# A band mask on the tensor engine: narrow local units of a four-layer attention kernel, with a re-searched instruction order

## The chip, the core and the metric

The kernel runs on one core of one Trainium2 chip. The core has a matrix engine (PE, with its weight loads shown apart as PEld), a vector engine (DVE), a scalar engine (ACT), a general engine (POOL) and a queue that issues transfers (SP). The metric is the device time of one execution in microseconds; smaller is better. Times are the median of the runs.

## The reference

Four layers act on one sequence of 2,048 tokens of 512 features: a local layer A, a global layer B, and both again with the same weights. Both have 32 heads of 16 features.

```
x = x + A(layernorm(x))      # A: W, dil = 8, 2: token i sees keys i, i-2, ..., i-14
x = x + B(layernorm(x))      # B: one shared K and V of 16 features, all 2048 keys, softmax
x = x + A(layernorm(x))
x = x + B(layernorm(x))

A: idx = pos[:, None] - arange(8) * 2;  logits = where(idx >= 0, q.k * 16**-0.5, -1e9)
   o = softmax(logits) @ v;  return o @ wo
B: return softmax(q @ k.T * 16**-0.5) @ v @ wo
```

The output has the shape and type of x, (1, 2048, 512) in bf16.

## The kernel before

**The global layers** are most of the work. Their scores are cut into 4,096 tiles of 128 keys by 512 queries. PE computes four tiles at a time, each on 32 of its rows (`score`, line 2534), and leaves them in PSUM. A tile then goes one of two ways. On the ACT way two tiles make one exponential (`exp`, line 2549, written to `pt`), and PE multiplies each by the values once. On the DVE way the tile is converted to integers (`copy`, line 2553, written to `t`), POOL makes two shifted versions of it (`do_pass`, line 2559, written to `i` and `i_pair`), and PE multiplies all three by scaled values. These products (`pv`, line 2570, written to `o`) use PE in four column strips side by side. So a tile on the ACT way costs PE one score and one product, and a tile on the DVE way one score and three products. There are two PSUM slots for scores on the ACT way, and at most two banks for scores on the DVE way.

**The local layers** are cut by token chunk (four chunks `c` of 512 tokens) and by half of a chunk (`kd`). Tokens of equal parity are neighbours, so the eight keys of a query lie in a band. The first two chunks of the first layer use wide units (72 key columns; they stay as they are). All others use narrow units: 48 of them, each with four heads on each 64-row half of PE, for eight blocks of 40 query columns, `UN` = 320 columns for each half. A narrow unit (`narrow_scores`) is 16 or 18 small score products into one PSUM slot (line 2455), one exponential on ACT (line 2463, written to `units`), and one AND on DVE that zeroes what lies outside the band (line 2469). In the first local layer every unit is finished by itself (`narrow_unit`). In the second, four units are finished together (`narrow_half`): PE sums the masked exponentials of the four (`total`, line 2386, written to `dn`), ACT takes the logarithm (line 2400) and an exponential (line 2402, both in `half`), the result goes out and back by transfer, and only then come the products with the values (line 2421). There are eight such groups.

**The order** of all instructions on all engines is fixed when the program is built. A planner (`Sched`, `Stream`) plays through the kernel with assumed durations (`MM`, `SWITCH`, `LAT`, the numbers given to `self.op`) and picks next what has the lowest key: its start plus weights. The weights are in `PRM`, `BIAS` and, for each of the 96 parts of the global layers, in the table `PHASES`. `FETCH` and `BLOCK` are the planner's limit on how fast PE gets its instructions. Each engine then runs its list in order and waits where data is missing. Where the plan leaves PE idle for long, it inserts products of zeros (`keep_awake`, line 1883).

Of the kernel before, what the change touches and what calls it, by code (L numbers as in the profile page):

```python
# [6 lines left out]
BF16 = mybir.dt.bfloat16  # L7
# [23 lines left out]
NJ = 3  # L31
# [379 lines left out]
def outproj_tm(ctx, tc, o_tm, wo_sb, x_sb, ident, S, tag):  # L411
# [5 lines left out]
    for qt in range(NT):  # L417
# [11 lines left out]
MM, SWITCH, DMA = 216.0, 96.0, 620.0  # L429
# [6 lines left out]
SENT, WALL, BLOCK, FETCH, REFILL = 45.0, 200.0, 255.55, 3050.0, 10.0  # L436
# [13 lines left out]
        "add": 223.2, "add_y": -114.7, "c2": -211.4, "c3": -91.88, "c6": 83.79, "c7": 14.68, "dve": -147.3,  # L450
        "ex": -306.6, "p0": -110.5, "sc": -133, "v1": -5823, "vcopy": 131.3, "vp": 291.7, "wpa": -0.02812,
    }, {
        "aq": -134.4, "dq": 158.3, "exq": -40.72, "mmi": 26.69, "mmq": 1.383, "nt": 46.85, "pv_in": 203.8,
        "slotv": -22.13, "vech": -0.2155,
    }, (77430, 20.0)),
    1: ({
        "act": 389.9, "add": 235.5, "add_y": -114.7, "c2": -211.4, "c3": -91.88, "dve": -147.3, "ex": -306.6,
        "p0": -110.5, "sc": -133, "vp": 291.7,
    }, {
        "aq": -134.4, "dq": 158.3, "exq": -40.72, "mmi": 26.69, "mmq": 1.383, "nt": 46.85, "open": 106.2,  # L460
        "pv_in": 203.8, "slotv": 1.595,
    }, (76143, 80.0)),
    2: ({
        "add": 235.5, "c0": -315, "c1": -201.2, "c3": -129.8, "c4": 4.013, "dve": -178.1, "evacX": 22.86, "ex": -306.6,
        "mm_b": -3091, "norm": 173.2, "recip": 151.1, "sc": -151.8, "see_b": 20390, "vp": 290.4, "wa": -0.1622,
    }, {
        "aq": -128.7, "dq": 159.2, "mmi": 51.61, "pv": 275.5, "vech": -0.2556, "vecp": -93.34,
    }, (48860, 160.0)),
    3: ({
        "add": 235.5, "c0": -315, "c1": -201.2, "c3": -129.8, "c4": 4.013, "dve": -178.1, "evacX": 22.86, "ex": -306.6,  # L470
        "mm_b": -3091, "norm": 173.2, "recip": 151.1, "sc": -151.8, "see_b": 20390, "vp": 290.4, "wa": -0.1622,
    }, {
        "aq": -128.7, "dq": 159.2, "mmi": 51.61, "pv": 275.5, "vech": -0.2556, "vecp": -93.34,
    }, (89741, 160.0)),
    4: ({
        "add": 96.11, "age": 0.03249, "c2": -189, "c6": 33.96, "evacX": 85.36, "ln": -136.1, "mask": 27, "mm_a": 202.8,
        "sc": -255.2, "turn": 31.66, "vcopy": 134.5, "vfirst": -1171,
    }, {
        "closing": 564.3, "few": 21.46, "mmi": 39.37, "ni": -30.74, "vec": 414.1,
    }, (95515, 160.0)),  # L480
    5: ({
        "aexp": -88.89, "age": 0.04278, "c1": -193.6, "c2": -145.8, "c4": -10.63, "c5": 114.5, "evac": 2514,
        "mm_b": -2741, "sc": -341.5, "turn_ev": -522.8, "wd": 0.03593, "wipe": 12860, "zer": -131.6,
    }, {
        "acth": 0.01482, "copy": 88.93, "dq": 10.2, "mmi": 48.87, "npt": 13.85, "pv_in": 70.63, "vecp": -61.26,
    }, (93829, 160.0)),
    6: ({
        "aexp": -88.89, "age": 0.04278, "c1": -193.6, "c2": -145.8, "c5": 114.5, "evac": 2514, "mm_b": -2741,
        "pad": -219200, "sc": -341.5, "turn_ev": -413.6, "wd": 0.03593, "wipe": 12860, "zer": -131.6,
    }, {  # L490
        "acth": 0.01482, "closing": 607.9, "copy": 88.93, "dq": 10.2, "mmi": 48.87, "npt": 13.85, "pv_in": 70.63,
    }, (11912, 160.0)),
    7: ({
        "aexp": -88.89, "age": 0.04278, "c1": -193.6, "c2": -145.8, "c5": 114.5, "evac": 2514, "mm_b": -2741,
        "pad": -219200, "sc": -341.5, "see": -217.3, "turn_ev": -413.6, "wd": 0.03593, "wipe": 12860, "zer": -131.6,
    }, {
        "acth": 0.01482, "closing": 607.9, "copy": 88.93, "dq": 10.2, "mmi": 48.87, "npt": 13.85, "pv_in": 70.63,
    }, (28948, 80.0)),
    8: ({
        "age": 0.05331, "away": -123.6, "c1": -362, "c6": 73.59, "dve": -144.6, "ln": -75.93, "mm_a": 399.4,  # L500
        "p0": -159.8, "pad": -219400, "see": -352.5, "st": -1643, "turn_ev": -423.9,
    }, {
        "aux": -5.231, "dq": 22.63, "mmi": 4.008, "mmpt": 17.28, "mmq": 13.92, "nt": 19.69, "pv": 282.5,
    }, (76363, 160.0)),
    9: ({
        "age": 0.05331, "away": -123.6, "c1": -362, "dve": -144.6, "mm_a": 399.4, "norm": 346.8, "pad": -219400,
        "see": -352.5, "st": -1643, "turn_ev": -423.9,
    }, {
        "copy": 73.55, "dq": 22.63, "mmi": 4.008, "mmpt": 17.28, "mmq": 13.92, "nt": 19.69, "pv": 282.5, "vecp": -61.45,
    }, (21942, 160.0)),  # L510
    10: ({
        "age": 0.05331, "c7": 39.95, "dmat": -84.43, "ln": -119, "on": 82.68, "p1": -6187, "recip": 124.2, "sc": -195.7,
        "split": -6952, "st": -1978, "turn": 52.13, "vcopy": 133.3, "vp": 61.75, "wpa": -0.01191,
    }, {
        "act": -83.47, "acth": -0.1093, "copy": 101.4, "mmi": 4.008, "mmpt": 12.19, "nt": -25.91, "pv": 216.7,
        "vecp": -57.25,
    }, (28571, 160.0)),
    11: ({
        "aexp": -73.39, "back": 1022, "c0": -186, "c3": -167.9, "dn": -21630, "mm_a": 222.2, "mm_b": -3007,
        "pad": -219500, "split": -7307, "turn_ev": -529.1, "v1": -5878, "wd": 0.189, "wpd": 0.1129, "zer": -389.9,  # L520
    }, {
        "aq": 19.81, "aux": -147.2, "mmi": -6.329, "pv": 195.3, "vec": 495.7, "vec2": 217.1, "vech": 0.1986,
    }, (63034, 8.0)),
    12: ({
        "back": 1023, "c0": -186, "c2": -182.3, "c6": 63.11, "dve": -78.77, "mm_a": 222.2, "mm_b": -3007,
        "split": -7428, "st": -1712, "v1": -5878, "wd": 0.09754, "wpd": -0.1118,
    }, {
        "aq": 19.81, "aux": -147.2, "exq": -79.78, "mmi": -6.329, "pv_in": 289.8, "vec": 517, "vec2": 147.3,
        "vech": 0.1395, "vecp": -52.17,
    }, (75059, 8.0)),  # L530
    13: ({
        "act": 248.2, "aggr": -3061, "away": -110.8, "c4": 8.258, "recip": 115.6, "split": -7535, "turn": 27.13,
        "v1": -6423, "vcopy": 152.3, "vp": 58.75, "wpa": -0.05655, "zer": -411.2,
    }, {
        "act": -142.3, "aq": -48.62, "few": 56.89, "pv_in": 207, "slotv": 35.96, "vech": -0.1282, "vecp": -65.6,
    }, (30282, 80.0)),
    14: ({
        "act": 248.2, "aexp": -50.83, "c1": -184.2, "c5": 142, "dmat": -59.08, "evacX": 72.81, "split": -7535,
        "turn": 27.13, "vcopy": 164.7, "wipe": 12740, "wpd": -0.06679,
    }, {  # L540
        "aq": -48.62, "aux": -8.007, "few": 56.89, "mmq": -15.71, "pv_in": 207, "slotv": 35.96,
    }, (33337, 160.0)),
    15: ({
        "add": 115.5, "age": 0.03159, "back": 144.4, "c7": 42.5, "dn": -21140, "dve": -56.65, "evac": 2855,
# [621 lines left out]
def act_ns(cols, pointers=0):  # L1166
    return 52.0 + 0.833 * cols + 93.0 * pointers
# [1888 lines left out]
```

## Time and profile before

| | |
|---|---|
| median of 3 runs | 1376.43 us (1375.53 to 1377.28) |
| the profiled execution | 1378.18 us, of which the span of the trace is 1376.0 us |
| mean granted clock of PE | 0.995 |
| busy | PE 97%, ACT 95%, DVE 93%, POOL 68% |

The rows further down are from the profiled execution. A busy PE is not a PE at its peak, since its products overlap; its pace is read from the starts of its instructions. The columns of a timeline are start and duration in microseconds, engine, line, operation, operands (out<-in), count, and in brackets the idle time before it and what ended it.

### The profile page before, as it was taken

To read this page: it belongs to the slowest core of one execution; us is meant where nothing else is said; L and a number is where in the kernel's file an instruction comes from. 1 tells how busy PE (TensorE), PEld (TensorE's weight loads), DVE (VectorE), ACT (ScalarE), POOL (GpSimd) and SP (SyncE) were. 2 spreads that over 40 slices of the span, in tenths; PEclk is the share of its full clock that TensorE was granted. 3 is DMA by queue.
4 is the path that set the end of the run, shared out by engine and by line. 5 is a ranking of instruction groups with operands and counts; after the bars stand their busy time and mean duration, and the time that the engine had idled before them with its cause. 6 is when DMAs were issued, how large, how long until landed. Compare 5 with 4: busy or idle time off the path is not lost. (4 is left out here: it accounts for less than half of the span.)

```text
span 1376.0 us, 48011 instructions
## 1 busy us (share of the span) xinstructions
PE 1341.6 (97%) x19604; PEld 459.4 (33%) x19606; DVE 1286.4 (93%) x2254; ACT 1311.4 (95%) x1549; POOL 929.2 (68%) x1226
## 2 busy tenths in 40 slices
PE   8999999999999999999999999999999999999997
PEld 5534243222223322433224334322222222222222
DVE  7987868999998899999998898999999999999998
ACT  6998989999999999999999998999999999999996
POOL 5126456787657567785677646877877678887884
PEclk9999999999999999999999999999999999999999
DMA  5012223011113110210113122221112200001000
GB/s 157 7 40 59 53 53 68 24 40 37 41 38 51 27 41 18 39 23 23 29 28 44 51 48 46 64 63 36 35 47 63 67 24 14 14 14 44 13 14 27
DMA packets 120876, 55.79 MB, mean 41 GB/s; under 512 B 98440, under 2 KB 104712, under 8 KB 120648
## 3 DMA queue, kind: packets, MB, share of 16 engines
q1 hardware_dynamic: 119784, 50.82, 15.9%
q8 instruction: 155, 2.54, 0.8%
q10 hardware_dynamic: 864, 1.84, 0.4%
q14 instruction: 73, 0.60, 0.1%
HBM read 27.10 MB, written 11.52 MB: 28 GB/s over the span
## 5 line engine op out<-in xcount | busy, mean ns | idle before, releaser
L2549 ACT ACTIVATE pt<-st 128x1024 bf16<-128x1024 f32 x1281 | 1196.3, 1121 | 27.1 <-PE dv L2534 12.3
L2553 DVE TENSOR_SCALAR t<-dv 128x512 int16<-128x512 f32 x1534 | 956.0, 680 | 34.0 <-PE dv L2534 24.7
L2559 POOL INT64_ADD i<-t x613 | 502.5, 825 | 245.5 <-DVE t L2553 102.3
L2559 POOL INT64_ADD i_pair<-t x411 | 337.7, 825 | 154.7 <-DVE t L2553 65.5
L2570 PE MATMUL o<-pt,VEa 128*32 128x512 bf16 x1308 | 260.7, 387 | 0.1
L2570 PE MATMUL o<-pt,region 128*32 128x512 bf16 x1254 | 259.6, 385 | 0.0
L2534 PE MATMUL st<-QT,KAB 32*128 32x512 bf16 x1308 | 255.0, 383 | 4.4 <-issue 1.2
L2534 PE MATMUL st<-QT,region 32*128 32x512 bf16 x1254 | 244.2, 380 | 8.5 <-ACT pt L2549 5.3
L2534 PE MATMUL dv<-QT,region 32*128 32x512 bf16 x794 | 241.2, 382 | 0.6 <-DVE t L2553 0.4
L2534 PE MATMUL dv<-QT,KAB 32*128 32x512 bf16 x740 | 235.5, 384 | 1.3 <-DVE t L2553 1.0
L2570 PE MATMUL o<-i,region 128*32 128x512 f16 x950 | 217.7, 385 | 0.1
L2570 PE MATMUL o<-t,region 128*32 128x512 f16 x794 | 208.6, 385 | 0.0
L2570 PE MATMUL o<-i,VEd 128*32 128x512 f16 x887 | 203.5, 385 | 0.1
L2570 PE MATMUL o<-t,VEd 128*32 128x512 f16 x740 | 193.9, 388 | 0.7 <-DVE t L2553 0.7
L2570 PE MATMUL o<-i_pair,region 128*32 128x512 f16 x638 | 168.8, 385 | 0.8 <-POOL i_pair L2559 0.8
L2534 PEld LDWEIGHTS <-region 32*128 32x128 bf16 x2048 | 82.4, 90 | 237.0 <-issue 233.3
L2534 PEld LDWEIGHTS <-KAB 32*128 32x128 bf16 x2048 | 79.6, 91 | 243.5 <-issue 238.5
L2570 PE MATMUL o<-i_pair,VEd 128*32 128x512 f16 x593 | 153.0, 384 | 0.0
L2570 PEld LDWEIGHTS <-region 128*32 128x32 f16 (+1 forms) x3636 | 71.7, 94 | 153.6 <-issue 149.4
L2570 PEld LDWEIGHTS <-VEd 128*32 128x32 f16 x2220 | 66.9, 94 | 83.4 <-issue 79.1
L2570 PEld LDWEIGHTS <-VEa 128*32 128x32 bf16 x1308 | 58.0, 94 | 60.7 <-issue 57.4
L2296 POOL COPY v<-xn 32x512 bf16<-32x512 bf16 x96 | 58.2, 606 | 11.0 <-DVE xn L1917 5.4
(205 smaller groups left out, 1085.8 us busy)
## 6 DMA issues: line engine op xcount, KB each, us to landing
xkd<-X SPq DMA_DIRECT2D x32, 256.0 KB
X<-xkd SPq DMA_DIRECT2D x32, 256.0 KB
lb<-rcd SPq DMA_DIRECT2D x31, 256.0 KB
shares<-lgd SPq DMA_DIRECT2D x8, 512.0 KB
X<-X SPq DMA_DIRECT2D x124, 32.0 KB
k<-oncA SPq DMA_DIRECT2D x96, 32.0 KB
w_sb<-in_A_wqkv_dram ACTq DMA_DIRECT2D x4, 384.0 KB
region<-in_A_x_dram SPq DMA_DIRECT2D x3, 512.0 KB
```

The lines of the kernel that those rows point to most:

```text
L2296: self.chain("pool", nc.gpsimd.tensor_copy(out=vv[rows, 4 * n:4 * n + 4, :, 16 * h:16 * h + 16].rearrange("p b g d -> p (b g) d"), in_=st. ...
L2534: self.chain("pe", self.nc.tensor.matmul(out, lhsT=self.KAB[l][32 * g:32 * g + 32, a, kt * 128:(kt + 1) * 128], rhs=self.QT[32 * g:32 * g ...
L2549: self.chain("act", self.nc.scalar.activation(out=self.pt[pt][:, 0:n, :], in_=self.st.pop(key)[:, 0:n, :], func=AF.Exp, scale=E_SCALE))
L2553: self.chain("dve", self.nc.vector.tensor_scalar(out=self.t[buf][:, r, :].bitcast(I16), in0=self.dv[bank][:], scalar1=-U_BIAS, scalar2=U_B ...
L2559: self.chain("pool", self.nc.gpsimd.int64_add(words(self.i[out]), words(self.t[buf]), J_OFF[j] * 0x0001000100010001))
L2570: self.chain("pe", self.nc.tensor.matmul(self.o[bank][32 * g:32 * g + 32, :], lhsT=lhsT, rhs=rhs, start=first, stop=last, tile_position=(0 ...
```

## The change

The AND of the 48 narrow units goes. In its place every narrow unit's scores begin with two products of 320 columns, one on each 64-row half, which write the band into PSUM: `copies` (made of identities) as weights, and `band` as moving data, which is 0 inside the band and -1e30 outside. The scores are then added to it in PSUM, and the exponential makes 0 of what lies outside. The 16 wide units keep their AND; its bits now lie in the spare part of the tile `half`. `band` and `copies` are built once, on DVE and POOL. Some of the planner's durations are other numbers (a narrow score 135 ns longer for the new products; others as they were measured), its fetch limit is 3,400 ns instead of 3,050, and `PHASES` is a newly searched table. The copy of the last key block (`keep`) now waits for all four of `k`, and two constants share a tile.

```diff
-MM, SWITCH, DMA = 216.0, 96.0, 620.0
+MM, SWITCH, DMA = 216.0, 98.0, 620.0
-SENT, WALL, BLOCK, FETCH, REFILL = 45.0, 200.0, 255.55, 3050.0, 10.0
+SENT, WALL, BLOCK, FETCH, REFILL = 45.0, 200.0, 255.55, 3400.0, 10.0
...
     0: ({
-        "add": 223.2, "add_y": -114.7, "c2": -211.4, "c3": -91.88, "c6": 83.79, "c7": 14.68, "dve": -147.3,
+        "add": 223.2, "add_y": -114.7, "away": -85.16, "c2": -211.4, "c3": -91.88, "c6": 83.79, "c7": 14.68,
...
-        t = 422.7 * n + 62
+        t = 421.0 * n + 62
...
+FAR_BELOW = 1e30
+    def make_band():
+        return nc.vector.tensor_scalar(out=band[:], in0=m[:, 0:NN], scalar1=-1.0, scalar2=FAR_BELOW, op0=ALU.add,
+                                       op1=ALU.mult)
+def build_copies(nc, out, ident):
+    nc.gpsimd.tensor_copy(out=out[:], in_=ident[:])
+    for a in (0, 64):
+        i = nc.gpsimd.tensor_copy(out=out[a:a + 64, 64 - a:128 - a], in_=ident[a:a + 64, a:a + 64])
+    return i
...
         def score(op):
             st = state["st"] = self.slot[op.buf].tile([128, 2, 512], F32, name="st")
             groups = [(g, slice(64 * g, 64 * g + 64)) for g in range(2)]
+            for g, gs in groups:
+                self.chain("pe", nc.tensor.matmul(
+                    st[:, g, 0:UN], lhsT=self.w.copies[gs],
+                    rhs=self.w.band[gs].unsqueeze(1).to_broadcast([64, UN // NN, NN]), start=True, stop=False,
+                    tile_position=(64 * g, 0), skip_group_check=True))
             for col, w, kx, _, q0 in parts:
                 for g, gs in groups:
                     self.chain("pe", nc.tensor.matmul(
-                        st[:, g, col:col + w], lhsT=kx[gs], rhs=qt[gs, qbase + q0:qbase + q0 + w], start=True, stop=True,
-                        tile_position=(64 * g, 0), skip_group_check=True))
+                        st[:, g, col:col + w], lhsT=kx[gs], rhs=qt[gs, qbase + q0:qbase + q0 + w], start=False,
+                        stop=col == parts[-1][0], tile_position=(64 * g, 0), skip_group_check=True))
...
-        sc = self.op("pe", 245.0, score, size=4 * len(parts), deps=[*deps, *P.prev], want=("slot", "exp"), solid=True, mode="row64",
+        sc = self.op("pe", 25.5 * len(parts) + MM * UN / 512, score, size=4 * len(parts) + 4,
+                     deps=[*deps, *P.prev, self.narrow_band, self.copied], want=("slot", "exp"), solid=True, mode="row64",
...
-        def mask(op):
-            x = P.t.bitcast(I32).rearrange("p (b c) -> p b c", c=NN // 2)
-            self.chain("dve", nc.vector.tensor_tensor(
-                out=x, in0=x, in1=self.w.band[1][:].unsqueeze(1).to_broadcast([128, 16, NN // 2]), op=ALU.bitwise_and))
-
-        return P.used(self.op("dve", 413.0, mask, [ex, self.narrow_bits], prio=("mask", *self.PRIO), port=("dve",)))
```

The order of the built programs shows two places at the last chunk of the second local layer, its second half. On DVE, in the program before, there stand a residual addition of the chunk's first half (`x_sb`), the statistics of its result, the four ANDs (`units`), and copies of tiles (`t`):

```order
L2498 TENSOR_TENSOR x_sb<-x_sb,y 128x512
L1965 BN_STATS sm_199<-x_sb 128x6
L2469 TENSOR_TENSOR units<-units,bandmask_103 128x320 x4
L2553 TENSOR_SCALAR t_160<-dv 128x512 x2
L2553 TENSOR_SCALAR t_161<-dv 128x512 x3
```

After the change, DVE from the same addition on:

```order
L2594 TENSOR_TENSOR x_sb<-x_sb,y 128x512
L2061 BN_STATS sm_198<-x_sb 128x6
L2649 TENSOR_SCALAR t_162<-dv 128x512 x2
L2649 TENSOR_SCALAR t_159<-dv 128x512
L2685 COPY X_168<-o 128x512
```

The four ANDs are gone, and copies of tiles stand next to each other. On ACT, before, the exponentials of the four units (`units`), those of global tiles (`pt`), and the logarithm and exponential of the four units' sums (`half`):

```order
L2549 ACTIVATE pt_158<-st 128x1024
L2463 ACTIVATE units<-st 128x640 x4
L2549 ACTIVATE pt_155<-st 128x1024
L2549 ACTIVATE pt_153<-st 128x1024
L2400 ACTIVATE half<-dn 128x256
L2549 ACTIVATE pt_152<-st 128x1024
L2402 ACTIVATE half<-half 128x256
```

And after:

```order
L2645 ACTIVATE pt_155<-st 128x1024
L2566 ACTIVATE units<-st 128x640 x4
L2497 ACTIVATE half<-dn 128x256
L2645 ACTIVATE pt_154<-st 128x1024
L2499 ACTIVATE half<-half 128x256
```

The logarithm has moved up: it stands right behind the exponentials of the units, where two exponentials of global tiles stood between. Over the whole program, this is so in 6 of the 8 groups after and in none before.

Counted over both whole programs, after against before: exponentials of global tiles 1,273 of two tiles and one of one, against 1,281 of two; copies on DVE 1,549 against 1,534; products with the values 7,194 against 7,164; zero products 182 against 199, with 4,832 columns fewer; evacuations of PSUM and similar copies of 512 columns 9 fewer on DVE and 9 more on ACT. Counted in passes of up to four side by side, PE's products with the values need 1,972 against 1,966 and its global scores 1,275 against 1,280. PE's list has a change between its row, column and other modes 2,576 times against 2,591. The narrow scores stand in 23 runs of one to four units against 22; units that are third or fourth in their run are 7 against 11.

## Rows read from the trace of the kernel before

**Rows 1.** The page, busy time of each engine.

```profile
PE 1341.6 (97%) x19604; PEld 459.4 (33%) x19606; DVE 1286.4 (93%) x2254; ACT 1311.4 (95%) x1549; POOL 929.2 (68%) x1226
```

**Rows 2.** Windows: busy us of each engine (count), granted clock, DMA share, GB/s.

```profile
0.00:135.00 135.00, 126.61 (x2901) 64.96 (x2903) 110.70 (x246) 114.12 (x195) 55.31 (x120) 0.99 0.24 65
...
434.00:767.00 333.00, 329.83 (x5192) 113.48 (x5191) 315.15 (x544) 323.99 (x369) 228.19 (x294) 1.00 0.17 32
767.00:862.00 95.00, 94.07 (x1671) 35.38 (x1671) 86.90 (x154) 87.85 (x102) 53.96 (x72) 1.00 0.25 53
862.00:1365.00 503.00, 493.23 (x5596) 145.94 (x5587) 496.85 (x832) 497.87 (x546) 391.49 (x485) 1.00 0.13 35
```

**Rows 3.** Timeline of PE, one cycle of global work alone.

```profile
1200.80 0.39 PE L2534 MATMUL st<-QT,region 32*128 32x512 bf16 x2
...
1201.14 0.39 PE L2570 MATMUL o<-pt,region 128*32 128x512 bf16 x2
...
1201.37 0.38 PE L2570 MATMUL o<-pt,region 128*32 128x512 bf16 x2
...
1201.72 0.39 PE L2534 MATMUL st<-QT,region 32*128 32x512 bf16 x2
```

**Rows 4.** Timeline of PE, one cycle with a projection.

```profile
824.92 0.39 PE L2534 MATMUL st<-QT,region 32*128 32x512 bf16 x2
...
825.25 1.05 PE L1942 MATMUL k<-xnT,w_sb 128*32 128x512 bf16 x16
826.22 0.39 PE L2534 MATMUL st<-QT,region 32*128 32x512 bf16 x2
```

**Rows 5.** Timeline of ACT behind that projection.

```profile
827.90 1.94 ACT L2549 ACTIVATE pt<-st 128x1024 bf16<-128x1024 f32 x2 [0.97 <-PE o L2570]
```

**Rows 6.** Groups by line and shape: busy us, mean ns, idle before them.

```profile
L2549 ACT ACTIVATE pt<-st 128x1024 bf16<-128x1024 f32 x1281 | 1196.3, 1121 | 27.1 <-PE dv L2534 12.3 <-PE o L2570 10.8 <-PE st L2534 0.9
L2553 DVE TENSOR_SCALAR t<-dv 128x512 int16<-128x512 f32 x1534 | 956.0, 680 | 34.0 <-PE dv L2534 24.7 <-PE st L2534 4.8
...
L2469 DVE TENSOR_TENSOR units<-units,bandmask 128x320 int32<-128x320 int32 x48 | 22.0, 487 | 12.8 <-ACT units L2463 4.2 <-POOL v L2296 3.8 <-POOL i_pair L2559 3.1
...
L1917 DVE CAST xn<-v 128x512 bf16<-128x512 f32 x20 | 13.8, 688 | 6.5 <-PE v L2280 3.1 <-POOL v L2296 3.0 <-DMA k<-oncA 0.3
...
L1914 ACT CAST oncA<-k 128x512 bf16<-128x512 f32 x8 | 4.7, 585 | 1.1 <-PE k L1942 1.1
```

**Rows 7.** Timeline of four narrow units scored in one run, to their sums.

```profile
868.98 0.37 PE L2455 MATMUL st<-q,k 64*128 64x40 bf16 x16
...
869.45 2.52 ACT L2463 ACTIVATE units<-st 128x640 bf16<-128x640 f32 x4
...
871.02 0.18 PE L2455 MATMUL st<-q,ks 64*128 64x8 bf16 x2
...
871.13 0.39 PE L2570 MATMUL o<-pt,region 128*32 128x512 bf16 x1
...
871.75 1.70 DVE L2469 TENSOR_TENSOR units<-units,bandmask 128x320 int32<-128x320 int32 x4 [0.57 <-POOL v L2296]
871.96 1.94 ACT L2549 ACTIVATE pt<-st 128x1024 bf16<-128x1024 f32 x2
...
872.67 0.49 PE L1883 MATMUL o<-zeros 128*32 128x512 bf16 x2
...
873.11 0.85 PE L2386 MATMUL dn<-units,heads 128*32 128x256 bf16 x16
...
874.00 0.38 ACT L2400 ACTIVATE half<-dn 128x256 f32<-128x256 f32 x1
```

**Rows 8.** Timeline of PE, two narrow units in one run, and two more.

```profile
839.64 0.37 PE L2455 MATMUL st<-q,k 64*128 64x40 bf16 x16
...
840.18 0.39 PE L2570 MATMUL o<-i_pair,region 128*32 128x512 f16 x1
...
841.50 0.19 PE L2455 MATMUL st<-q,k 64*128 64x32 bf16 x2 [0.28 <-issue]
```

More of the change, by code (lines that the diff above doesn't have):

```diff
@@ new lines @@
+    59: ({
+        "add": 155.7, "aexp": -44.09, "aggr": -3219, "away": -79.19, "back": 310.2, "c1": -183, "c3": -191.3,
+        "c4": 6.654, "mask": -14.78, "on": 66.77, "sc": 263.8, "score": -147.9, "spread": -54.08, "st": -1947,
+        "v0": 943.1, "v1": -6642, "wd": 0.302, "wipe": 12900, "wpd": -0.06787,
+    }, {
+        "act2": 4391, "batch": 20.02, "late": -8.023, "mmpt": 5.11, "mmq": 14.3, "ni": -13.39, "npt": 0.8339,
+        "open": 309.7, "pv_in": 136.2, "slotv": -2.099, "vec2": 178.7, "vecp": -56.58,
+    }, (65210, 40.0)),
@@ new lines @@
+        "mask": 45.88, "mm_a": 411.1, "norm": 178.6, "p0": -142.6, "split": -7504, "v0": 1593, "vp": 58.7,
+        "wipe": 12480,
+    }, {
+        "aq": -125.3, "aux": 39.25, "batch": 22.72, "closing": 1439, "dq": 10.16, "exq": -41.21, "few": 7.404,
+        "late": -34.39, "mmi": 30.31, "mmpt": 54.33, "mmq": 6.584, "ni": -44.11, "npt": 32.7, "nt": -40.24,
+        "open": 571.1, "pv": 295.7, "pv_in": 180.4, "vec": 446.8, "vec2": 291.8, "vech": -0.2135, "vecp": -63.63,
+    }, (51719, 160.0)),
@@ L1011 @@
[L1011 to L1022 removed]
+    }, (61220, 20.0)),
@@ new lines @@
+    86: ({
+        "act": 418, "aexp": -71.01, "age": 0.04371, "aggr": -3494, "back": 162.1, "c4": 1.823, "c6": 50.88, "c7": 8.517,
+        "dmat": -165.8, "ln": -124.2, "recip": 343.1, "score": -381, "turn_ev": -514.7, "vcopy": 149, "vp": 48.81,
+        "wa": -0.1263, "zer": -265.4,
+    }, {
+        "act2": 4315, "acth": -0.1096, "aux": -7.726, "batch": 20.31, "dq": 19.81, "exq": -116.9, "ni": -5.188,
+        "nt": -8.533, "open": 724.6, "slotv": 4.44, "vec2": 139.4,
+    }, (19901, 160.0)),
@@ L1663, with build_band_mask @@
 UN = 8 * NN
-def build_band_mask(nc, cpool, m):
-    bits = [cpool.tile([128, n // 2], I32, name=f"bandmask{n}") for n in (NQ, NN)]
+FAR_BELOW = 1e30
+def build_band_mask(nc, cpool, m, bits):
+    band = cpool.tile([128, NN], BF16, name="band")
     def select(keys):
@@ L2351, in dn @@
                         start=False, stop=False, skip_group_check=True, tile_position=(0, 32 * r)))
-        p0 = self.op("pe", 250.0, pv, [ms, *v, *extra], size=8 * len(parts), solid=30.0, mode="col", sub="all", prio=("p0", *self.PRIO),
+        p0 = self.op("pe", 29.0 * len(parts), pv, [ms, *v, *extra], size=8 * len(parts), solid=30.0, mode="col", sub="all", prio=("p0", *self.PRIO),
                      want=("bank", "aux"))
```

1182 lines of the change are left out of this document (619 added, 563 removed), and 12 rows, old and new, of the table PHASES.

## Prediction

> **What bounds the kernel now.** I read the page first: PE, ACT and DVE are busy 97%, 95% and 93% of the span [rows 1], so no engine alone explains the time, and an average over the span hides which one decides where. The windows part it. In the last 503 us, global work almost alone, ACT is busy 497.9 and DVE 496.9 [rows 2]: both are full, and only less work on both shortens that stretch. From 434 to 862 us, where the second local layer is made beside global work, ACT has 9.0 + 7.2 = 16.2 us idle and DVE 17.9 + 8.1 = 26.0, while PE's rows hardly leave a gap. In the first 135 us all three have idle time. The narrow units stand in the second kind of stretch and at the end of the first kind.
>
> The timeline tells why PE decides there. A cycle of global work runs from one score pass to the next in 0.92 us [rows 3]: 0.34 for scores and a change of mode, 0.23 for a first pass of products, 0.35 for a second and the change back. It feeds ACT two tiles, which are 1196.3 / 1281 = 0.93 us of ACT's time [rows 6]. So here PE and ACT go at one pace. With a projection in it the cycle takes 1.30 us for the same two tiles [rows 4], and ACT, with only two slots of scores ahead, runs dry: 0.97 us in the place shown [rows 5]. In these stretches a microsecond more or less on PE counts; a microsecond on DVE counts only if tiles can move to it.
>
> **What the change does, engine by engine.**
>
> DVE: the 48 ANDs were busy 22.0 us, 0.46 each [rows 6]. Fifteen more tiles come, at 956.0 / 1534 = 0.62 us: +9.3. Nine evacuations of 0.69 go: -6.2. Sum -18.9 us.
>
> ACT: eight exponentials of 0.93 go and one of half the size comes: -7.0. Nine evacuations of 0.585 come: +5.3. Sum -1.7 us. So the order gives ACT back, in other work, most of what it takes from it, and DVE's relief is mostly not spent.
>
> PE has six terms.
> (a) The band. A pass of 512 columns takes 0.23 us [rows 3], so 320 columns take 0.14 if the two halves go side by side, and 0.29 if not. Two units, 18 pairs together, took 0.54 us with a change of mode of 0.34 - 0.23 = 0.11 [rows 8], or 24 ns for a pair; at 0.23 us for 512 columns one product of 40 columns is 18 ns, so one after the other would be 36 ns a pair. They go side by side. 48 x 0.144 = +6.9; bounds 0 (all of it under the wait for a slot) and 13.8.
> (b) Units that are third or fourth in their run wait for a slot. Four units took 871.13 - 868.98 = 2.15 us [rows 7], two took 0.54 [rows 8]: (2.15 - 1.08) / 2 = 0.53 for each late unit, paced by unit exponentials of 2.52 / 4 = 0.63. The order has 7 late units for 11: -2.1. In the 7 that remain the band lies inside the wait: 7 x 0.144 = -1.0.
> (c) Fifteen changes of mode fewer at 0.11: -1.6. One pass more in all (six more of products, five fewer of scores): +0.2.
> (d) Instruction supply. PE sits 0.28 us on "issue" between two narrow products [rows 8], where hundreds of small instructions follow each other. The plan now assumes a slower supply and can put other work there. There are 12 groups of four units; bounds 0 and 12 x 0.28 = -3.4; I take half, -1.7, since only the new durations, not a removed instruction, speak for it, and each unit sends four instructions more.
> (e) Idle time that the plan fills with zero products: 4,832 columns fewer, at 0.23 us for 512: -2.2; by the order they go from the first sixth of the 96 parts, where work waits for results rather than for an engine.
> (f) The sums of the eight groups of the second local layer. Before, they waited for the ANDs: 1.70 us on DVE from 871.75 on, and PE filled 873.11 - 872.67 = 0.44 with zeros before it began the sums [rows 7]. If this simply goes, -3.5 for eight. But the ANDs' time was covered: two exponentials of global tiles ran on ACT meanwhile (1.94 us, [rows 7]). After the change the logarithm stands right behind the unit exponentials in 6 of 8 groups, as the order shows. So PE waits for the last unit exponential instead: from 871.13 to 871.96, 0.83 us, of which a pass of products covers 0.23; and ACT waits from there to the logarithm, which began 874.00 - 873.11 = 0.89 us after the sums did. What is queued behind the waiting logarithm are the exponentials of global tiles, whose scores PE too sends only after the sums. The removed wait and the new one are about equal on PE (0.44 against 0.60). I take 0; bounds -3.5, and 6 x 0.89 = +5.3 if ACT's idle time counts in full.
>
> PE's sum: 6.9 - 2.1 - 1.0 - 1.6 + 0.2 - 1.7 - 2.2 = -1.5 us. ACT's, -1.7, lies in the same stretches and isn't added; by the order none of the exponentials that go stands in the last third of the 96 parts, where ACT is full. POOL gets ten more adds at 68% busy [rows 1], and loses the ANDs as something that it waits for: nothing on the path. The build of `band` and `copies` is three small copies and one conversion long before the first narrow unit: nothing.
>
> **The forecast** is therefore 1.6 us less. The profiled execution took 1378.18 us for a span of 1376.0; it lies 1.75 above the median of the runs, so I carry the difference, not the level: 1376.43 - 1.6 = 1374.8 us. That is within 0.2% of the time before (2.75 us, about what a measurement of this kernel can tell from no change).
>
> **The rivals.**
> *The waits shrink more than I allow.* The sums lose their wait in full (-3.5) and the supply stalls go (-1.7 more): 1374.8 - 5.2 = 1369.6. For it: the chain from unit exponential to sums is 1.70 us shorter in each group. Against it: the logarithm's new place.
>
> *PE has room, and DVE's relief is worth its full price.* If only ACT and DVE bound the kernel, tiles could move until both save the same: (18.9 - 1.7) / (0.62 + 0.47) = 15.8 tiles more, and both would be 1.7 + 15.8 x 0.47 = 9.1 us shorter, 1367.3. For it: both are full in the last 503 us [rows 2]. Against it: the order moves 15 tiles, not 31, and the cycle with a projection shows PE setting the pace [rows 4, 5]. The Trainium skill (Perfetto Trace Analysis, section Identifying the Most-Contended Engine) has a rule that speaks for this rival: the busy share of matmuls is no measure of PE's headroom, the share of weight loads is, and the engine with the highest occupancy comes first. The weight loads are 33% here [rows 1], so by that rule PE would take the band for nothing and ScalarE with VectorE would decide; the time would then be this rival's. The cycles of 0.92 and 1.30 us speak against it, because the change of mode and the passes fill them though the weight loads don't.
>
> *Slower: the new wait decides.* The logarithm behind the unit exponentials holds up ACT by 0.89 us in 6 groups, +5.3, and PE, which sends no scores meanwhile, doesn't make it up: 1380.1. If the late units' gain (b) is lost as well, as every unit now fills its slot 0.14 us later, 1383.2. It decides as soon as ACT's idle time in 434 to 862 us grows beyond the 16.2 us that it has. For it: ACT and PE go at one pace, so a hole on ACT is not given back by cycles of 0.92 against 0.93. Against it: in those stretches ACT is idle anyway.
>
> *The change does not do what it says.* That the ANDs go and the products come is seen in the order; only their price is open, which the bounds of (a) hold.
>
> **How the numbers follow.** My forecast 0.42, the first rival 0.20, the second 0.12, the slower one 0.26. The forecast's own range is 1372 to 1378.5; a seventh of it lies below 1373.7. So faster 0.38, same 0.36, slower 0.26. For 8 times in 10 the range takes in the second rival's time at its lower end and most of the slower one's: 1367 to 1381.5.
>
> **What would show it in the profile after.** (a) Each pair of band products starts within a few ns, and the first scores follow 0.13 to 0.15 us later; a unit in a two-unit run takes some 0.41 us instead of 0.27. (b) A run of four units still takes about 2.2 us. (f) Idle time of ACT in front of the logarithm, put down to the sums, grows from what it is to some 4 or 5 us; PE fills the time before the sums with zeros or sits. DVE is busy about 1267 us, ACT about 1310. Idle time of ACT from 434 to 862 us is 13 to 20 us. Wrong I am if PE's rows show the band at 0.29 us, if ACT's idle time in the narrow stretches falls by over 4 us (a gain that the order's counts don't show), or if the last 503 us change by more than 1%.

## The result, and the profile after

The changed kernel takes 1385.41 us (median of 4 runs, 1383.17 to 1385.94) against 1376.24 for the kernel before (1375.53 to 1377.28): ratio 1.0063, 95% interval 1.0046 to 1.0080. It is slower by 9 us, where 1.6 us less was forecast. The profiled execution took 1385.17 us, its span is 1383.4 us, its mean granted clock 0.989.

The busy times came out as forecast (DVE 1267, ACT 1310). The page of the changed kernel, busy time of each engine, answers to [rows 1]:

```profile
PE 1344.3 (97%) x19715; PEld 467.7 (34%) x19715; DVE 1269.9 (92%) x2211; ACT 1310.0 (95%) x1552; POOL 938.6 (68%) x1239
```

So the loss isn't work. I cut both programs where every eighth of the 96 parts of the global layers leaves PSUM. Time in us at which a part ends:

| part | 8 | 32 | 56 | 64 | 96 | span |
|---|---|---|---|---|---|---|
| before | 134.9 | 434.4 | 862.4 | 977.4 | 1364.8 | 1376.0 |
| after | 151.5 | 446.8 | 862.2 | 983.9 | 1371.9 | 1383.4 |
| after, with the start of before | 142.3 | 436.6 | 851.9 | 972.8 | 1361.3 | 1373.0 |

The changed kernel loses 16.6 us in the first eight parts, and gains 4.2 from there to the 32nd part and 5.9 from there to the 64th; the rest is 0.9 slower. Not all of the 16.6 us is loss: the new order also does more within the first eight parts (768 products `oa` for 724, 192 `y` for 160, 43 `dv` for 37 in the traces), and with the start of before, where it does the same, the eighth part still ends 7.4 us later. Its windows, cut at the 8th, 32nd, 48th, 56th and 96th part (busy us of each engine and count, granted clock, DMA share, GB/s), answer to [rows 2]:

```profile
0.00:151.50 151.50, 138.83 (x2993) 70.56 (x2993) 111.69 (x248) 118.78 (x207) 60.18 (x128) 0.92 0.22 58
446.80:775.50 328.70, 326.29 (x5234) 114.42 (x5230) 310.36 (x533) 319.34 (x364) 232.70 (x299) 1.00 0.16 31
775.50:862.20 86.70, 86.38 (x1250) 28.40 (x1251) 80.15 (x143) 83.89 (x96) 50.46 (x66) 1.00 0.20 49
862.20:1371.90 509.70, 499.21 (x6028) 152.48 (x6020) 497.74 (x829) 503.60 (x555) 394.71 (x490) 1.00 0.14 36
```

In the first window the granted clock is 0.92 where it was 0.99, and PE has 12.7 us without work where it had 8.4. In the stretch with the second local layer, ACT's idle time fell to (328.70 - 319.34) + (86.70 - 83.89) = 12.2 us from 16.2.

What happens at the start stands in the timeline of POOL, DVE and PE. In the changed kernel:

```profile
12.85 6.18 PE L2210 MATMUL v<-w_sb,xnT 128*32 128x256 bf16 x128 [0.91 <-ACT xnT L2118]
...
19.31 1.27 POOL L2228 COPY v<-oncA 64x512 bf16<-64x512 bf16 x2
20.65 1.43 POOL L1759 TENSOR_SCALAR_AFFINE_SELECT half<-half 32x8 bf16<-32x8 bf16 x7
...
22.65 1.29 POOL L1761 TENSOR_SCALAR_AFFINE_SELECT half<-half 32x32 bf16<-32x32 bf16 x6
24.00 1.28 POOL L2228 COPY v<-oncA 64x512 bf16<-64x512 bf16 x2
25.31 0.41 DVE L2101 TENSOR_SCALAR pt<-region,sm 128x512 bf16<-128x512 bf16 x1 [3.09 <-POOL v L2228]
...
28.74 1.90 PE L2038 MATMUL q<-xnT,w_sb 128*32 128x512 bf16 x16 [2.63 <-DVE QT L2118]
```

In the kernel before:

```profile
17.16 1.27 POOL L2132 COPY v<-oncA 64x512 bf16<-64x512 bf16 x2
18.47 0.41 DVE L2005 TENSOR_SCALAR pt<-region,sm 128x512 bf16<-128x512 bf16 x1 [1.37 <-POOL v L2132]
18.50 1.53 POOL L1673 TENSOR_SCALAR_AFFINE_SELECT half<-half 32x8 bf16<-32x8 bf16 x7
...
20.60 1.28 POOL L1675 TENSOR_SCALAR_AFFINE_SELECT half<-half 32x32 bf16<-32x32 bf16 x6
21.94 1.28 POOL L2132 COPY v<-oncA 64x512 bf16<-64x512 bf16 x2
...
22.82 1.05 PE L1942 MATMUL k<-xnT,w_sb 128*32 128x512 bf16 x16 [1.04 <-ACT QT L2022]
```

The selects on POOL build the narrow mask and run ahead of the last pair of copies of `v` in both kernels; from the first to the last they take 3.4 us before and 3.3 after. DVE's last normalisation of the second chunk (`pt`) stands ahead of this pair in the order before, and behind it after the change. So there DVE waits 3.09 us, and PE 2.63 us in turn.

### The profile page after: what moved, and what is told of

It is laid out like the page before. It is cut to its first block, busy times and chain, and to the rows that moved or that the text cites. A ratio compares the mean times of both kernels' runs of the same rounds, so it can differ in the third digit from the quotient of the medians.

```text
span 1383.4 us, 48181 instructions
## 1 busy us (share of the span) xinstructions
PE 1344.3 (97%) x19715; PEld 467.7 (34%) x19715; DVE 1269.9 (92%) x2211; ACT 1310.0 (95%) x1552; POOL 938.6 (68%) x1239
## 3 DMA queue, kind: packets, MB, share of 16 engines
q8 instruction: 156, 2.56, 0.8%
## 4 chain that ended last, share of the span: by engine, by line
PE 70%; ACT 19%; DVE 4%; issue 3%; POOL 2%; DMA 1%; DVEq 0%; SPq 0%; POOLq 0%; ACTq 0%
PE o L2666 29%; PE st L2630 23%; ACT pt L2645 18%; PE y L2038 3%; PE qb L2038 2%; PE k L2038 2%; PE q L2038 2%; PE dv L2630 2%; PE v L2377 1%; DVE t L2649 1%; PE o L1979 1%; POOL i L2655 1%; PE st L2557 1%; PE oa L2518 1%; PE st L2551 1%
## 5 line engine op out<-in xcount | busy, mean ns | idle before, releaser
L2649 DVE TENSOR_SCALAR t<-dv 128x512 int16<-128x512 f32 x1549 | 967.3, 683 | 42.5 <-PE dv L2630 37.0
L2655 POOL INT64_ADD i<-t x622 | 509.2, 825 | 232.3 <-DVE t L2649 79.3
L2630 PE MATMUL st<-QT,KAB 32*128 32x512 bf16 x1293 | 252.0, 382 | 8.7 <-ACT pt L2645 4.0
L2666 PE MATMUL o<-pt,VEa 128*32 128x512 bf16 x1293 | 254.8, 386 | 0.0
L2666 PE MATMUL o<-i,region 128*32 128x512 f16 x951 | 221.9, 385 | 0.6 <-POOL i L2655 0.6
L2666 PE MATMUL o<-t,VEd 128*32 128x512 f16 x755 | 197.7, 385 | 0.1
```

The costliest lines, as they stand in the source:

```text
L2630: self.chain("pe", self.nc.tensor.matmul(out, lhsT=self.KAB[l][32 * g:32 * g + 32, a, kt * 128:(kt + 1) * 128], rhs=self.QT[32 * g:32 * g ...
L2649: self.chain("dve", self.nc.vector.tensor_scalar(out=self.t[buf][:, r, :].bitcast(I16), in0=self.dv[bank][:], scalar1=-U_BIAS, scalar2=U_B ...
L2655: self.chain("pool", self.nc.gpsimd.int64_add(words(self.i[out]), words(self.t[buf]), J_OFF[j] * 0x0001000100010001))
L2666: self.chain("pe", self.nc.tensor.matmul(self.o[bank][32 * g:32 * g + 32, :], lhsT=lhsT, rhs=rhs, start=first, stop=last, tile_position=(0 ...
```

## Experiments

The 18 runs stand in one table (20 rows with the two kernels). Ratio: to the kernel before on the same chip; its median lies between 1376.24 and 1377.51 us on the chips used, so a difference between two rows is good to about 1 us. Stops: gaps of over 0.6 us between the starts of two successive PE instructions (products and weight loads together) at whose end the trace names nothing that was waited for, count and sum, without the last 15 us of the program. The last column is the span less these stops.

| kernel | median us | ratio, 95% | part 8 | span | stops | rest |
|---|---|---|---|---|---|---|
| before | 1376.24 | | 134.9 | 1376.0 | 4, 3.5 | 1372.5 |
| after | 1385.41 | 1.0063 (1.0046-1.0080) | 151.5 | 1383.4 | 3, 4.4 | 1379.0 |
| old_order_band | 1387.84 | 1.0083 (1.0069-1.0098) | 134.2 | 1386.2 | 10, 11.3 | 1374.9 |
| new_order_and | 1420.74 | 1.0322 (1.0306-1.0337) | 149.9 | 1418.6 | 6, 7.1 | 1411.5 |
| new_old_start | 1374.74 | 0.9983 (0.9975-0.9992) | 142.3 | 1373.0 | 3, 2.7 | 1370.3 |
| old_new_start | 1387.99 | 1.0073 (1.0060-1.0086) | 144.3 | 1387.3 | 4, 2.9 | 1384.4 |
| new_start15 | 1383.98 | 1.0050 (1.0032-1.0068) | 149.0 | 1381.9 | 3, 3.7 | 1378.2 |
| new_held | 1379.21 | 1.0018 (1.0010-1.0027) | 145.4 | 1376.8 | 4, 4.2 | 1372.6 |
| new_start15_held | 1379.22 | 1.0018 (1.0007-1.0030) | 143.6 | 1374.2 | 4, 4.0 | 1370.2 |
| new_swap | 1381.39 | 1.0028 (1.0016-1.0040) | 145.9 | 1378.5 | 5, 4.9 | 1373.6 |
| old_held | 1379.02 | 1.0011 (1.0002-1.0020) | 136.7 | 1377.3 | 6, 5.1 | 1372.2 |
| new_old_start_held | 1377.42 | 1.0000 (0.9991-1.0009) | 143.3 | 1375.9 | 2, 2.4 | 1373.5 |
| new_late_mask | 1375.76 | 0.9994 (0.9985-1.0003) | 141.4 | 1372.1 | 3, 3.0 | 1369.1 |
| old_late_mask | 1377.31 | 1.0003 (0.9994-1.0012) | 134.8 | 1374.7 | 5, 5.0 | 1369.7 |
| new_zeros | 1386.51 | 1.0068 (1.0055-1.0081) | 149.6 | 1383.3 | 8, 8.8 | 1374.5 |
| new_zeros_warm | 1387.65 | 1.0074 (1.0055-1.0092) | 149.9 | 1386.0 | 10, 11.0 | 1375.0 |
| new_old_start_warm | 1379.19 | 1.0011 (1.0003-1.0020) | 143.9 | 1376.8 | 7, 6.5 | 1370.3 |
| new_old_start_noband | 1382.32 | 1.0043 (1.0028-1.0057) | 140.7 | 1379.6 | 7, 8.9 | 1370.7 |
| new_old_start_twice | 1387.14 | 1.0075 (1.0059-1.0091) | 144.1 | 1385.8 | 10, 10.7 | 1375.1 |
| old_order_tiny | 1391.87 | 1.0105 (1.0086-1.0124) | 134.3 | 1388.8 | 11, 12.6 | 1376.2 |

Eight of the 18 times lie over 1 us outside every range that was expected of them: old_order_band, new_order_and, new_swap, old_held, new_old_start_held, new_old_start_warm, new_old_start_noband and old_order_tiny. The eighth part of new_old_start, expected at 135 to 141 us, ended at 142.3.

**Each half of the change alone.** The first kernel keeps the order before, takes the 48 ANDs out and puts the band in; the second has the changed kernel's order, without the band and with an AND behind each narrow exponential.

```diff
 # old_order_band
-        self.chain("dve", nc.vector.tensor_tensor(out=x, in0=x, in1=..., op=ALU.bitwise_and))
+        pass
...
+            for g, gs in groups:
+                self.chain("pe", nc.tensor.matmul(st[:, g, 0:UN], lhsT=self.w.copies[gs], rhs=..., start=True, stop=False, ...))
 # new_order_and
+        ex.then = lambda op: self.sched.note(op.end + LAT["act"], mask)
```

> The order of the kernel before, instruction for instruction, with the 48 ANDs left out and the 96 band products (with the three copies that build them) put in: the mechanism alone. Theory 1 (the loss of the changed kernel lies in the first eight parts, in the order that was searched anew; the band itself costs a few us of PE at most): 1373 to 1379 us, the eighth part ends at 134.9 us as before. Theory 2 (the loss is the band on PE, 6.9 us and more, and the wait of the logarithm behind it): 1381 to 1386 us, and the first eight parts as before.

> The order of the changed kernel, instruction for instruction, with the band products and their copies left out and the 48 ANDs put back on VectorE behind their exponentials: the order and the plan's new numbers alone. Theory 1: the loss stays, 1383 to 1390 us, the eighth part ends near 151 us. Theory 2: the loss goes, 1375 to 1379 us.

The band alone costs the old order 11 us, though DVE has 20 us less to do; the AND in the place of the band costs the new order 35. Neither theory expected these times. In the latter, at the sums of four units (timeline of DVE, PE and ACT):

```profile
930.15 0.49 DVE L2567 TENSOR_TENSOR units<-units,band 128x320 int32<-128x320 int32 x1 [1.06 <-POOL i L2659]
930.69 0.72 PE L2482 MATMUL dn<-units,heads 128*32 128x256 bf16 x16 [4.06 <-DVE units L2567]
...
931.46 0.38 ACT L2496 ACTIVATE half<-dn 128x256 f32<-128x256 f32 x1 [4.96 <-PE dn L2482]
```

DVE is held by POOL, PE's sums wait 4.06 us for the AND and ACT 4.96 us for the sums; over the program PE waits here 18.0 us in 10 places. The new order has its place for the logarithm because no AND stands in the chain: order and band are one change, and neither half shows its worth alone.

**The start.** Here the planner's choices are replaced by a list; the list is the kernel's own except for its beginning, the first 62 us of the plan or the first 15 us, which comes from the other kernel.

```diff
-        self.sched.plan()
+        self.sched.replay(json.loads(zlib.decompress(base64.b85decode("".join(SCRIPT)))))
```

> The changed kernel, with the first 62 us of its plan (365 steps, all of them ahead of the first global score) taken from the plan of before and everything behind in its own order. Theory 1: the eighth part ends 10 to 16 us earlier, at 135 to 141 us instead of 151.5, and the time is 1369 to 1376 us, under both kernels. Theory 2: 1384 to 1386 us, as the narrow units are untouched.

> The kernel before (its ANDs, its order) with the first 62 us of its plan taken from the changed kernel's plan, and that plan's rule that the spill copy waits for all keys. Theory 1 (the loss is the start's order by itself): 1385 to 1389 us, the eighth part 8 to 12 us later than 134.9. Rival (the start is slow only together with the band, by its copies and conversion on GpSimd and VectorE): 1376 to 1379.

> The changed kernel with the first 15 us of its plan from the plan of before, which lets the first products of v begin with the first transposed tile instead of the last. The products began 1.7 us later in the changed kernel, at half the clock until 17 us. If that is what the held building left over (7 us of the start): 1377 to 1380. If the products of v have room behind them: 1383 to 1386.

The start alone turns the verdict: with that of before the changed kernel is 10.7 us faster than as it was given, and 2.2 us faster than the kernel before; the new start costs the kernel before 11 us. Only the first 15 us (the order of the first products of `v`) bring 1.4, which the intervals don't tell from nothing.

To ask whether it is the selects, 17 building instructions on POOL are held until their place in the plan, behind the copies of `v`:

```diff
-lambda op: self.chain("pool", w.select(32))
+lambda op: w.select(32, lambda i: self.chain("pool", i))
```

> The changed kernel, with each of the 17 instructions on GpSimd that make the narrow mask held in the order of the plan (32 us or later), where only the last of them was held and the others slipped between the copies of v at 19 to 24 us. Theory 1a (the start loses because the last pair of those copies, and VectorE's norm that is chained behind it, stand behind 3.4 us of mask building; PE then idles 2.6 us and runs at the lower clock until 35 us): the hole at 26 us and the lower clock behind it go, 1376 to 1381 us. Theory 1b (the start loses through its order as such: the first products of v wait for the last transposed tile): under 2 us, 1383 to 1385. Theory 2: no change, 1385.

> The same first 15 us, and the mask building held at its planned place. If the two add: 1373 to 1376 us. If the building only moves its cost from 20 us to 34 us: 1377 to 1379, no better than the held building alone (1379.2).

> The kernel before with the mask building held at its planned place, a control. If the 3.4 us of building hurt only the new order's start: 1376 to 1377.5, no change. If they hurt any start: 1371 to 1374, and what holding them gained in the changed kernel (6.2 us) was no part of the change's loss.

> The changed kernel with the first 62 us of its plan from the plan of before, and the mask building on GpSimd held at its planned place as well. If the old start escapes the mask building because VectorE's norms stand ahead of the last pair of copies in it: 1373.5 to 1375, no more than 1.2 us under the 1374.7 of the old start alone. If the building costs every order alike: 1369 to 1371.

Timeline of POOL, DVE and PE of new_held:

```profile
17.35 2.56 POOL L2228 COPY v<-oncA 64x512 bf16<-64x512 bf16 x4 [0.26 <-DVE sm L2079]
...
19.95 0.41 DVE L2101 TENSOR_SCALAR pt<-region,sm 128x512 bf16<-128x512 bf16 x1 [0.37 <-POOL v L2228]
...
23.70 1.05 PE L2038 MATMUL q<-xnT,w_sb 128*32 128x512 bf16 x16 [0.24 <-DVE QT L2118]
```

The copies run through, the norm comes at 19.95 instead of 25.31, PE's hole is 0.24 us instead of 2.63, and the kernel is 6.2 us faster. Where the norm stands ahead anyway, holding gains nothing (old_held +2, new_old_start_held +2.7). The other way to the same end moves one instruction: the norm goes ahead of the pair of copies.

```diff
-    ["pool", "qkv vcopy c0#0"], ... ["dve", "ln norm c1#0"],
+    ["dve", "ln norm c1#0"], ["pool", "qkv vcopy c0#0"], ...
```

> The changed kernel with one step of its plan moved: VectorE's norm of the last quarter of the second chunk stands ahead of the last pair of copies of v on GpSimd, as in the kernel before, and no longer behind it and the mask building; on VectorE that is one instruction, one place earlier than the conversion of k. If it was this place that made PE idle 2.6 us at 26 us: the time falls as with the held building or more, 1376 to 1380 us. If the loss is spread over the whole start: 1384 to 1386.

That gains 4.0 us: its norm starts at 20.57, its `q` products at 25.27. Built from 50 us on, mask, copies and constants free the start altogether:

> The changed kernel with the old start (1374.7 us as it stands), and the building of the narrow mask and of the ones, heads and copies moved on GpSimd to 50 us and later, where GpSimd has nothing to do until 75 us. If the building is in the way of the copies of v wherever it stands before 50 us (held at its planned 33 us it cost 2.7 us with this start, and slipping between the copies it may cost something too): 1371 to 1374. If it costs nothing with the old start, where it slips in: 1374 to 1376.

> The kernel before with the same move. In the way: 1373 to 1376 us, as many us less as in the changed kernel. Not in the way: 1376 to 1378.

Neither differs measurably from its kernel without the move; with the norm in the right place the selects harm nobody.

**The clock or the wait.** PE's hole is followed by a granted clock of 0.50 from 30 to 35 us, the lower of its two levels (1.2 and 2.4 GHz). Zero products fill the hole at 26 us, and in a second kernel also the hole of 2.50 us ahead of the first transposes.

```diff
 # new_zeros, ahead of the second chunk's last q
+                for _ in range(12):
+                    self.idle_matmul(spare[:, 0, :], (128, 32), 512, True)
 # new_zeros_warm, new_old_start_warm
-        for _ in range(17):
+        for _ in range(26):
             self.idle_matmul(warm, (128, 128), 512, True)
```

> The changed kernel with twelve products of zeros (512 columns each, 0.21 us at the full clock) put into the hole of 2.6 us at 26 us, ahead of the product that waits there. The wait itself stays. If the lower clock from 28.7 to 35 us follows from that idle time and matters: 1382 to 1384 us, 1.5 to 3.5 under the changed kernel, and the granted clock of 30 to 35 us is 1.00 instead of 0.50. If only the wait matters: 1385 to 1386.

> The changed kernel with the twelve zero products in PE's hole at 26 us, and nine more zero products of 512 columns in the hole of 2.50 us ahead of its first transposes (10.06 us). If the lower granted clock of the start (0.50 from 11 to 18 us and from 28 to 35 us) is what the changed kernel loses, it now goes: the first v products take 3.7 us instead of 6.18, the 8th part of the global work ends about 145 us and the time is near 1379. If the waits behind POOL's select instructions set the end, the clock shows 1.00 and the time stays within 1.5 us of 1385.4 and of the 1386.5 of the twelve zeros alone.

> The changed kernel with the start of the kernel before, and the same nine zero products ahead of PE's first transposes. If its runs lose time to a lower clock at the start, their median falls from 1374.7 by up to 2 us and their mean granted clock rises from 0.995; if the clock there is hidden, the time stays within 1 us of 1374.7.

Windows of 10 us, the changed kernel:

```profile
10.00:20.00 10.00, 8.96 (x170) 6.42 (x174) 5.29 (x17) 6.21 (x15) 3.20 (x7) 0.66 0.62 148
20.00:30.00 10.00, 7.37 (x137) 3.65 (x132) 6.10 (x15) 7.35 (x14) 5.69 (x20) 0.91 0.36 122
30.00:40.00 10.00, 10.00 (x315) 7.33 (x311) 7.32 (x15) 7.57 (x17) 2.44 (x4) 0.75 0.03 7
```

And new_zeros_warm:

```profile
10.00:20.00 10.00, 8.69 (x215) 6.23 (x219) 6.93 (x18) 8.69 (x18) 4.85 (x13) 1.00 0.60 149
20.00:30.00 10.00, 9.32 (x178) 4.95 (x174) 6.50 (x17) 6.58 (x14) 4.07 (x13) 1.00 0.38 123
30.00:40.00 10.00, 9.76 (x382) 7.37 (x376) 9.02 (x17) 9.20 (x21) 4.47 (x7) 1.00 0.04 10
```

From 10 to 40 us the clock is at its upper level, and still part 8 ends at 149.9, only 1.6 us earlier, and the kernel isn't faster. The twelve zeros alone (new_zeros) brought the clock to 1.00 from 20 to 40 us, part 8 to 149.6 and no time either. The wait has stayed (timeline of PE, new_zeros_warm):

```profile
23.52 2.78 PE L1979 MATMUL st<-zeros 128*32 128x512 bf16 x12
26.93 1.05 PE L2043 MATMUL q<-xnT,w_sb 128*32 128x512 bf16 x16 [0.63 <-DVE QT L2123]
```

The `q` products start at 26.93, against 23.70 in new_held, whose profiled execution has the same clock of 1.00 up to 40 us; its part 8 ends 4.5 us earlier. The account isn't clean: before part 8 the kernel with the zeros has 3.9 us of stops and the changed kernel 1.2, so that the clock may be worth up to 1.6 + 2.7 = 4.3 us at the start; and against new_held (1.5 us of stops) 2.4 of the 4.5 us are stops, which leaves 2.1 for the wait. Nine zero products in idle time also made new_old_start 4.4 us slower, though nothing waits for them; its stops grew from 2.7 to 6.5 us.

**The price of the band, and of instructions as such.** Three kernels: the band left out of new_old_start, whose narrow units then have no mask at all, the band sent twice, and in the kernel before two zero products of 16 columns per narrow unit, as many instructions as the band with a twentieth of its columns.

```diff
 # new_old_start_noband: the two band products go, and
+                        st[:, g, col:col + w], ..., start=True, stop=True,
 # new_old_start_twice
-            for g, gs in groups:
+            for g, gs in groups * 2:
 # old_order_tiny
+                self.chain("pe", nc.tensor.matmul(st[:, g, 0:16], lhsT=self.w.zeros[gs], rhs=..., start=True, stop=True, ...))
```

> The changed kernel with the old start and without the band products (and without ANDs: the narrow units are not masked), so that PE has 192 instructions less; the order stays. The band's price in its own order: if it is mostly hidden there (under waits for slots, and the plan paced the supply for it), 1371.5 to 1374.5; if it costs what it cost in the old order, a unit 0.13 us and the stops of the supply, 1364 to 1369.

> The changed kernel with the old start and each band product sent twice (the second writes over the first): 96 products more at the same places. At 0.13 us for each of 48 units: 1381; with stops of the instruction supply as in the old order with the band: 1383 to 1387; if PE has room there: 1375 to 1378.

> The kernel before (its order, its ANDs) with two products of zeros of 16 columns ahead of each narrow unit's scores, where the band's stand in the run of the old order with the band: as many instructions more on PE (192 with their weight loads), but 32 columns a unit instead of 640. If the band's cost in the old order (10.9 us) is its 0.13 us of columns a unit: 1377 to 1378.5. If a good part is the supply of instructions, whose stops move when instructions are added ahead of them: 1380 to 1385.

All three are slower, the one that does less too, and the tiny products cost more (15 us) than the real band (11). Where it goes shows at the products of a finished unit with the values (`oa`), 64 in a row. Timeline of PE, before:

```profile
757.22 0.67 PE L2421 MATMUL oa<-units,v 128*32 128x40 bf16 x64
```

In old_order_band:

```profile
764.33 0.63 PE L2433 MATMUL oa<-units,v 128*32 128x40 bf16 x59
766.34 0.21 PE L2433 MATMUL oa<-units,v 128*32 128x40 bf16 x5 [1.38 <-issue]
```

In old_order_tiny:

```profile
766.59 0.63 PE L2421 MATMUL oa<-units,v 128*32 128x40 bf16 x59
768.20 0.21 PE L2421 MATMUL oa<-units,v 128*32 128x40 bf16 x5 [0.98 <-issue]
```

Both stop behind the same product, the 59th, and wait for nothing that the trace shows. In new_old_start_noband another such row:

```profile
874.30 0.19 PE L2987 MATMUL oa<-units,vs 128*32 128x8 bf16 x3
876.95 0.17 PE L2987 MATMUL oa<-units,vs 128*32 128x8 bf16 x1 [2.46 <-issue]
```

Now the table's last column. For 16 of the 20 kernels the span less the stops lies between 1369.1 and 1376.2 us, while the spans go from 1372.1 to 1388.8. The four outside have the wait at the start (after, new_start15, old_new_start) or the wait for the ANDs; the two changed kernels with zeros have the wait at the start too and lie in the upper part of the range. So of old_order_band's longer span of 10.2 us 11.3 - 3.5 = 7.8 are stops, of old_order_tiny's 12.8 it is 9.1, of new_old_start_twice's 12.8 (against new_old_start) 8.0, and of new_old_start_noband's 6.6 it is 6.2. The changed kernel's own loss isn't of this kind: 0.9 us of stops, 6.5 of rest.

## Why the prediction was wrong

The measured 1385.41 us lies above the forecast's range, above the wide one (1367 to 1381.5) and above every rival.

**The step that failed** is a term that the sum doesn't have: the start. The prediction looked at the first sixth of the parts under (e) alone, as a place "where work waits for results rather than for an engine", and credited it 2.2 us for fewer zero products. The new search had also reordered the first 62 us of the plan, and that costs 10.7 us (new_old_start). Shown is: the norm behind POOL's copies, these behind 3.3 us of selects, then DVE's 3.09 and PE's 2.63 us. Taking that away alone gives 4.0 us (the norm moved) or 6.2 (the selects held); the order of the first `v` products gives nothing that is clear of noise, by itself (1.4) or on top of the held selects. The remaining 4.5 us between new_held and new_old_start aren't settled. The lower clock goes with PE's holes; keeping it up with zeros doesn't bring the time back, but its own share, up to 4.3 us, isn't parted cleanly from the wait. The signs stood in the trace of before: DVE's norm already waited 1.37 us for POOL at 18.47, with the selects next in POOL's list at 18.50. A comparison of the two orders at this place is what the prediction lacks.

**The rest of the sum** held in sign. With the old start the change is worth 1376.93 - 1374.74 = 2.2 us against 1.6 forecast (the terms add up to 1.5). That the size agrees is luck in good part: by stretches this kernel's profiled execution is 7.4 us later at the eighth part, gains 5.2 to the 32nd and 6.8 to the 64th and loses 1.6 behind it, which no term of the sum says; and leaving the band out or sending it twice made the kernel 8 and 12 us slower, for the most part through PE's stops.

(a) and (b), the band: right. The changed kernel's two-unit run answers to [rows 8] (timeline of PE):

```profile
865.24 0.31 PE L2551 MATMUL st<-band,copies 64*128 64x320 bf16 x2
865.38 0.35 PE L2557 MATMUL st<-q,k 64*128 64x40 bf16 x16
...
865.61 0.30 PE L2551 MATMUL st<-band,copies 64*128 64x320 bf16 x2
...
866.05 0.39 PE L2630 MATMUL dv<-QT,region 32*128 32x512 bf16 x1
```

Scores follow 0.14 us behind the band; two units take 0.81 us instead of 0.54, 0.135 each. A run of four takes 895.67 - 893.32 = 2.35 us ("about 2.2"), of which [rows 7] had 2.15: in late units most of the band lies inside the wait. All narrow score phases together take 29.5 us instead of 26.1: 3.4 against 6.9 - 2.1 - 1.0 = 3.8 (28.1 us with the old start).

(c) Fifteen changes of mode fewer: so it is in the trace (2,577 against 2,592). (d) Supply: the term is of the right kind, since the 0.28 us of [rows 8] stand at one of the block ends described in the last section, but it counts the wrong thing, groups of units, and has the wrong size: a gain of 1.7 us was forecast, with bounds of 0 and 3.4, and the stops went from 3.5 to 4.4 us, or to 2.7 with the old start; these runs span 2.4 to 12.6 us of stops.

(f) The sums: the run of four in the changed kernel (timeline of PE and ACT):

```profile
893.32 0.31 PE L2551 MATMUL st<-band,copies 64*128 64x320 bf16 x2
...
893.88 2.64 ACT L2566 ACTIVATE units<-st 128x640 bf16<-128x640 f32 x4
...
895.67 0.39 PE L2666 MATMUL o<-i,region 128*32 128x512 f16 x1
...
896.56 0.46 PE L2483 MATMUL dn<-units,heads 128*32 128x256 bf16 x16
...
897.08 0.38 ACT L2497 ACTIVATE half<-dn 128x256 f32<-128x256 f32 x1 [0.57 <-PE dn L2483]
```

ACT's wait ahead of the logarithm is 0.57 us here, 3.4 us in 6 over the program (1.6 in 3 before); forecast 4 to 5. The sums start 3.24 us behind the run's begin, before 4.13. This is where the order lives from the missing AND, as new_order_and shows with its 18.0 us. From part 32 to 64 the changed kernel is 5.9 us faster, more than my terms for that stretch. Two of my own signs of error did come: ACT's idle time there fell by 4.0 us, just at the bound of 4, and the stretch behind the 56th part grew by 1.5%. But 6.7 of its 7.3 us lie between the 56th and the 64th part, to which the order has moved local work; behind that it is 388.0 us against 387.4.

**"The build: nothing"** isn't quite what the trace shows. Timeline of DVE and POOL, the changed kernel:

```profile
46.80 1.90 DVE L1769 TENSOR_SCALAR band<-half 128x40 bf16<-128x40 bf16 x1
46.86 1.81 POOL L2324 MEMSET k<- 128x2048 f32 x1
```

The conversion of 40 columns takes 1.90 us, as long as POOL's memset beside it; in new_zeros the same instruction took 0.17 us. What this cost the kernel no run shows. The Trainium skill (SBUF — State Buffer, section SBUF: two separate sides) says that GpSimd (POOL) and a VectorE (DVE) instruction in a mode with two ports share a pair of ports as an exclusive lock for a whole instruction, so that the other engine fully blocks; the trace agrees in the length of the conversion, but doesn't tell its mode.

**The rivals.** That the waits shrink more (1369.6) didn't come. That PE has room (1367.3) didn't come either: even with the old start the kernel takes 1374.74 us. Old_order_band, with 96 products more on PE, 20 us less on DVE and 11 us more in all, speaks against it but doesn't settle it, because its order is fixed and 7.8 us of its longer span are stops. The Trainium skill (Perfetto Trace Analysis, section Identifying the Most-Contended Engine) has the share of weight loads among its measures of PE's headroom; that share, 33% before and 34% after, gave no sign of these stops, and the rival that it spoke for came out wrong. The slower rival had nearly the sign and size, 1380.1 to 1383.2, but another cause: the wait ahead of the logarithm grew by 1.8 us, and in the stretch named the kernel became faster.

## What to carry to other kernels

When a change brings a newly searched order, compare the orders where the engines wait most, at the start above all, for every instruction that now stands behind another engine's unplanned work; a sum over operations doesn't see it. Try the change with the old order's beginning before judging it. And where PE runs tens of thousands of small instructions, count its unexplained stops in both traces first, and look whether they stand at every 256th instruction: here instructions alone, used or not, moved the time by more than the work in question.

## What was unexpected

PE's stops go by the count of instructions. Numbered from 0 in order of time, products and weight loads together, PE's records fall into blocks of 256, and all 115 stops of the 20 kernels stand at the end of such a block: the record behind the stop has a number that is 192 or 193 more than a multiple of 256. Each stop ends 1.2 to 1.6 us after a packet of one queue has landed, which the profile lists for instructions, here in the changed kernel (packets, MB, share):

```profile
q8 instruction: 156, 2.56, 0.8%
```

156 packets of 2.56 MB / 156 = 16.4 KB, for 2 x 19,715 PE instructions: an estimate of one packet for some 250, which fits a block. And in 112 of the 115 cases PE had run through the block ahead of the stop in under 3.5 us, where the median of all other blocks is 10 us. So PE stops where a dense block is over before the next one is there. This isn't the whole rule: behind 222 other blocks of under 3.5 us no such stop stands, and what sets them apart no run here shows. The planner has the same limit in `BLOCK` (255.55 instructions) and `FETCH`.

With that the odd results fall into place. An instruction more or less, used or not, moves every later block end to another place in the work. Old_order_band and old_order_tiny, with different work at the same count, stop at the same product; nine idle products put first cost 4.4 us; 192 small instructions (96 products with their weight loads) cost 15 us, and leaving 192 out cost 7.6. A change of this size can't be judged by its work alone.
